# The first attention tiles laid out anew: query quarters on ScalarE's queue, keys without doubling, constants and norms moved, two value products brought forward

## The chip, the cores and the metric

The kernel runs on one core of one Trainium2 chip. The metric is the device time of one execution in microseconds (us); several executions are timed and the median is compared. The core has TensorE (PE, matmuls; its weight loads are listed as PEld), VectorE (DVE), ScalarE (ACT), GpSimd (POOL) and SyncE (SP, which only issues DMAs here). Each engine takes its instructions in program order, and waits on semaphores for other engines and for DMAs.

## What is computed

Three layers follow each other: attention with pooled keys and values, a mixture of experts with top-1 routing, and a maximum of three products with an output product. The change touches the attention alone.

```python
B, H, S, D = 8, 8, 576, 64
Sp = S // 8                                   # 72 pooled keys a head
k_p = k.reshape(B, H, Sp, 8, D).mean(axis=3)
v_p = v.reshape(B, H, Sp, 8, D).mean(axis=3)
scores = np.matmul(q, k_p.transpose(0, 1, 3, 2)) / np.sqrt(D)
attn = softmax(scores)
x = np.matmul(attn, v_p)                      # -> 4608 tokens x 512
xn, en = x / norm(x), expert_emb / norm(expert_emb)
expert = argmax(xn @ en.T / tau)              # then relu(x @ w1[e]) @ w2[e], gated
out = max(y @ m1, y @ m2, y @ m3) @ mo        # y: the gated result
```

## The kernel before

The 4608 tokens are 36 tiles of 128 tokens, nine for two batches; the fifth of the nine holds 64 tokens of each of the two. A loop over `it` in `attention_moe_moe_kernel` runs the tiles as a pipeline written out by hand: in iteration `it` it issues the scores of tile it-1 (`stage_s`, L474, for a mixed tile L460; then VectorE's maximum L489 and subtraction L492), the transposes of exp of tile it-3 (`stage_a`, L505), the query transposes of tile it (`stage_q`, L449), the exp of tile it-1 (`stage_e`, L498), squares of finished rows (L561), and the value products of tile it-4 (`stage_x`, L528, with VectorE's normalisation L538 to L555). After that come the jobs that `todo[it]` lists. Every engine keeps this order, so a job that waits holds up all that stands behind it on its engine.

The jobs prepare a batch's keys and values (`prep_steps`). A batch's 576 pooled rows lie in five pieces of 128, 128, 128, 128 and 64 rows; for keys that are aligned to heads the fourth and fifth have 120 and 72. `pool_k` sums eight rows on VectorE (L300), `pool_k2` does it in three halving steps on GpSimd (L314), `pool_v` and `pool_v1` do the same for values (L324 on GpSimd, L308 on VectorE). `dup_k` writes the keys a second time beside themselves on ScalarE (L318). `trans_k` transposes the pieces on TensorE (L342), and ScalarE copies them into the block-diagonal `kbd` (L346, L347). `spread_v` places the values into `vbd` on GpSimd (L330), `trans_v` transposes them (L376, copied at L378), and `vdot` multiplies them with the normalised expert vectors (L383, then L390 on VectorE). From batch 2 on `trans_kv` transposes keys and values together (L354). From batch 3 on only half of each group of eight rows is loaded, and `add_half` (L207) adds the other half with an adding DMA from GpSimd's queue.

All first loads are issued by SP, in the order expert vectors, keys of batch 0, half the heads of the first queries, values of batch 0, other half, and so on (L245 to L252); the buffers for raw keys and values hold two batches, so a later load waits until a batch has been summed. The PSUM tiles for scores, transposed exp and value products are single, two more (`pq`) serve all other transposes.

The constant steps and the expert vectors' norm are generators whose steps `fill` puts between VectorE's instructions of a tile:

```python
queue.append([chain(en_steps())])
p0[1]()
todo = {0: [lambda: fill(16), p0[2]], 1: [lambda: fill(2), p0[3]], 2: [p0[4]], 3: [p0[5]], 5: [lambda: queue.append([chain(const_steps())])]}
```

Behind the attention follow the routed experts and the last products, both mostly on TensorE.

## Time and profile before

| | |
|---|---|
| median of 3 runs | 1225.17 us (1224.39 to 1225.65) |
| the profiled execution's own time | 1225.17 us |
| span of its profile | 1223.3 us |
| TensorE busy | 98% of the span |
| VectorE, ScalarE, GpSimd busy | 65%, 47%, 25% |

The span goes from the first to the last instruction; the time around it is 1.9 us. "Busy" counts the union of an engine's instructions. Rows of a timeline give the start and the length in us, the engine, the line, the operation with its tiles, how many were merged (x8), and in brackets the idle time before with what ended it. Rows of a table by stretch give for each engine the busy time and the number of instructions, then the granted TensorE clock, the mean share of the 16 DMA engines and GB/s.

### The profile page before, as it was taken

What the parts mean: (1) busy time and instruction counts of PE and PEld (TensorE: products, weight loads), DVE (VectorE), ACT (ScalarE), POOL (GpSimd) and SP (SyncE); (2) the same over time, 40 slices, a digit from 0 to 9 for tenths busy, and PEclk for the clock granted to TensorE, in tenths of its full rate; (3) what the DMA queues carried; (4) which work ended last, traced back from release to release, by engine and by line L of the source; (5) the groups of instructions that cost most, each with busy time, mean ns of one, the idle gap of its engine ahead of it and who ended that gap; (6) DMA issues with size and microseconds to landing.
All of it is one profiled execution on the core that took longest, in us unless ns stands there. A gap on an engine that the chain in (4) does not pass through costs nothing. (4 is left out here: it accounts for less than half of the span.)

```text
span 1223.3 us, 22433 instructions
## 1 busy us (share of the span) xinstructions
PE 1194.4 (98%) x8251; PEld 1149.6 (94%) x8251; DVE 791.5 (65%) x1601; ACT 578.9 (47%) x1040; POOL 308.9 (25%) x441
## 2 busy tenths in 40 slices
PE   6899999999999999999999999999999999999998
PEld 5899999999999999999998998998998998998996
DVE  6878977987799899987844445445455454454450
ACT  4666764455666666666654223323323223223221
POOL 6977734301122121230002102003003003004001
PEclk9999999999999999999999999999999999999999
DMA  9999655418875447555359565574574674674631
GB/s 266 255 255 247 177 185 178 131 20 224 269 254 184 150 166 254 210 180 161 116 157 342 207 241 207 198 249 190 213 250 183 218 258 170 229 262 158 241 144 54
DMA packets 104134, 246.21 MB, mean 201 GB/s; under 512 B 17436, under 2 KB 69962, under 8 KB 95954
## 3 DMA queue, kind: packets, MB, share of 16 engines
q1 hardware_dynamic: 84786, 183.19, 44.1%
q0 software_dynamic: 19232, 61.52, 16.8%
q8 instruction: 67, 1.10, 0.4%
q14 instruction: 49, 0.40, 0.1%
HBM read 252.23 MB, written 46.98 MB: 245 GB/s over the span
## 5 line engine op out<-in xcount | busy, mean ns | idle before, releaser
L1658 PE MATMUL p<-yhi,wt 128*128 128x384 f32 x1512 | 387.6, 336 | 0.5 <-DVE m L1679 0.4
L1658 PEld LDWEIGHTS p<-yhi,wt 128*128 128x128 f32 x1512 | 273.4, 188 | 1.5 <-DVE m L1679 0.7
L1658 PE MATMUL p<-ylo,wt 128*128 128x384 f32 x756 | 254.2, 336 | 0.0
L1666 ACT COPY s<-p 128x384 f32<-128x384 f32 x162 | 77.6, 480 | 222.1 <-PE p L1658 217.6
L1142 PE MATMUL py<-hhi,wlo 128*128 128x256 f32 x576 | 163.2, 283 | 1.6 <-DVE wlo L1074 1.6
L1142 PE MATMUL py<-hhi,whi 128*128 128x256 f32 x576 | 164.7, 286 | 0.0
L1094 PE MATMUL ph<-xhi,whi 128*128 128x256 f32 x576 | 163.9, 285 | 0.7 <-DVE hlo L1110 0.7
L1094 PE MATMUL ph<-xhi,wlo 128*128 128x256 f32 x576 | 163.2, 283 | 0.7 <-DVE wlo L1074 0.7
L1094 PE MATMUL ph<-xlo,whi 128*128 128x256 f32 x576 | 163.1, 283 | 0.0
L1142 PE MATMUL py<-hlo,whi 128*128 128x256 f32 x576 | 163.0, 283 | 0.0
L1658 PEld LDWEIGHTS p<-ylo,wt 128*128 128x128 f32 x756 | 142.2, 188 | 0.5
L1687 DVE TENSOR_TENSOR blk<-p,s 128x384 f32<-128x384 f32 x108 | 59.7, 553 | 112.4 <-PE p L1658 112.4
L1643 POOL DMA_INDIRECT gt<-gbuf,ix x26 | 37.5, 1444 | 308.0 <-DMA ix<-idbuf 301.6
L1142 PEld LDWEIGHTS py<-hhi,wlo 128*128 128x128 f32 x576 | 110.4, 192 | 1.8 <-DVE wlo L1074 1.8
L1094 PEld LDWEIGHTS ph<-xhi,whi 128*128 128x128 f32 x576 | 110.6, 192 | 1.2 <-DVE hlo L1110 1.0
L1094 PEld LDWEIGHTS ph<-xhi,wlo 128*128 128x128 f32 x576 | 110.6, 192 | 0.9 <-DVE wlo L1074 0.9
L1094 PEld LDWEIGHTS ph<-xlo,whi 128*128 128x128 f32 x576 | 110.6, 192 | 0.0
L1142 PEld LDWEIGHTS py<-hlo,whi 128*128 128x128 f32 x576 | 110.5, 192 | 0.0
L1142 PEld LDWEIGHTS py<-hhi,whi 128*128 128x128 f32 x576 | 110.5, 192 | 0.0
L1074 DVE TENSOR_TENSOR wlo<-w2raw,whi 128x1024 fp32r<-128x1024 f32 x84 | 102.3, 1222 | 9.2 <-ACT whi L1072 9.2
L1074 DVE TENSOR_TENSOR wlo<-w1raw,whi 128x1024 fp32r<-128x1024 f32 x67 | 81.9, 1223 | 27.9 <-ACT whi L1072 27.0
L1072 ACT CAST whi<-w2raw 128x1024 fp32r<-128x1024 f32 x88 | 91.7, 1042 | 7.5 <-PE py L1142 4.7
(326 smaller groups left out, 2255.1 us busy)
## 6 DMA issues: line engine op xcount, KB each, us to landing
wt<-wdram SPq DMA_DIRECT2D x51, 1792.0 KB
w1raw<-in_moe_w_dram SPq DMA_DIRECT2D x88, 512.0 KB
w2raw<-in_moe_w_dram SPq DMA_DIRECT2D x88, 512.0 KB
wdram<-wst POOLq DMA_DIRECT2D x9, 1792.0 KB
ybuf<-yo SPq DMA_DIRECT2D x40, 256.0 KB
cvraw<-in_moe_w_dram POOLq DMA_DIRECT2D x36, 256.0 KB
xbuf<-x SPq DMA_DIRECT2D x16, 512.0 KB
yr<-ybuf SPq DMA_DIRECT2D x20, 384.0 KB
```

The lines of the kernel that those rows point to most:

```text
L1072: nc.scalar.copy(hi, src)
L1074: eng.tensor_tensor(lo, src, hi.bitcast(F32), op=A.subtract)
L1094: nc.tensor.matmul(ps[:, f, :], a_[:, c, fs], b_[:, c, :], start=(n == 0), stop=(n == 3 * DC - 1))
L1142: nc.tensor.matmul(py[:, c // 2, (c % 2) * 256 : (c % 2 + 1) * 256], a_[:, f, c * P : (c + 1) * P], b_[:, f, :], start=(piece == 0 and f = ...
L1643: nc.gpsimd.indirect_dma_start(out=gt[g][:, j : j + 1], out_offset=None, in_=gbuf[:, :], in_offset=bass.IndirectOffsetOnAxis(ap=cols[j], a ...
L1658: nc.tensor.matmul(ps, a_, b_, start=(start and c + n == 0), stop=(c == 1 and n == 2), skip_group_check=True)
L1666: nc.scalar.copy(t, ps)
L1687: tt(src, add[0], add[1], op=A.add)
```

## The change

- The expert vectors, the first two query quarters (tiles 0 and 1 of heads 0 to 3, then of heads 4 to 7) and `tau` are issued on ScalarE's queue; SP issues keys, values, and then the queries' other half. The last query group is loaded in two halves, around batch 1's values.
- Keys are transposed without being doubled; both copies into `kbd` read the same 64 PSUM rows. Tile 0 needs only three pieces and the first four heads; the others follow behind its scores. The first keys use the value products' PSUM tile.
- Batch 2's keys are summed three pieces on GpSimd and two on VectorE, and transposed apart from its values; batch 3's adding DMAs are issued behind batch 2's sums of the same kind. Batch 1's first value piece is summed on VectorE.
- Most clears move from VectorE to ScalarE, the first `kbd`'s from GpSimd to VectorE; masks and the other clears of `kbd` come in iteration 2. Most of the norm's steps go to GpSimd. Seven constant steps come first, the others from iteration 8 on.
- In iterations 5 and 6 the exp transposes and value products of the older tiles are issued before the new tile's scores, with batch 1's key transposes between them in iteration 5.

```diff
-        def inverse_norm(pool, ss, n, cols, pre_, tg=None):
+        def inverse_norm(pool, ss, n, cols, pre_, tg=None, eng_=nc.vector):
...
             for _ in range(3):
-                nc.vector.tensor_tensor(t, yf, yf, op=A.mult)
+                eng_.tensor_tensor(t, yf, yf, op=A.mult)
...
+            def load_first(t0, hs, eng):
+                if (0, 0) not in qg:
+                    qg[0, 0] = qp.tile([P, H, 4, D], F32, tag="qgrp", name="qgrp0_0")
+                eng.dma_start(
+                    qg[0, 0][:, hs, t0 : t0 + 2, :].rearrange("p h t d -> p h (t d)"),
+                    q[0, hs, 0:512].rearrange("h (p t) d -> p h (t d)", t=4)[:, :, t0 * D : (t0 + 2) * D],
+                )
...
-            nc.sync.dma_start(en, emb)
+            nc.scalar.dma_start(en, emb)
+            for hs in (slice(0, HP), slice(HP, H)):
+                load_first(0, hs, nc.scalar)
+            nc.scalar.dma_start(rtau, tau.rearrange("(o t) -> o t", o=1).partition_broadcast(P)[:, 0, :])
             kv[0] = [load_rows("kraw", k, 0, KC, True)]
-            load_q(0, 0, lambda: kv[0].append(load_rows("vraw", v, 0, RC, step=2)))
+            kv[0].append(load_rows("vraw", v, 0, RC, step=2))
+            load_first(2, slice(0, H), nc.sync)
             load_q(0, 1)
             kv[1] = [load_rows("kraw", k, 1, KC)]
-            load_q(0, 2)
+            load_q(0, 2, ((0, 2),))
             kv[1].append(load_rows("vraw", v, 1, RC))
...
+            nc.scalar.activation(esq, en, AF.Square, accum_out=ess)
...
+            nc.vector.memset(kbds[0], 0.0)
+            clear(vT[0:D])
+            clear(vT[D:P, 4, R4:P])
+            clear(enT[0:D])
+            clear(vps[0][R4:P, 4, :])
+            clear(aTs[0][R4:P, 4, :])
+            clear(vbds[0][R4:P, SL[4] : NSL, :])
+            clear(aTs[1][R4:P, 4, :])
...
-                vp = kp[:, :, 1, :] if b > 1 else vps[b]
+                vp = kp[:, :, 1, :] if b > 2 else vps[b % 2]
...
+                def first_k():
+                    ps = pb.tile([P, 2, 512], F32, tag="pav", name="ptk0")
+                    flat = ps.rearrange("p a n -> p (a n)")
+
+                    def heads(cs, parts):
+                        for c in cs:
+                            n, col = KC[c], c * P if c < 4 else 512
+                            nc.tensor.transpose(flat[0:D, col : col + n], kp[0:n, c, 0, :], ident[0:n, 0:n])
+                        for h0, h1, col in parts:
+                            src_ = flat[0:D, col : col + (h1 - h0) * SP].rearrange("p (h s) -> p h s", s=SP)
+                            nc.scalar.copy(kb[0:D, h0:h1, 0, :], src_)
+                            nc.scalar.copy(kb[D:P, h0:h1, 1, :], src_)
+
+                    return (
+                        lambda: heads(range(3), ((0, 4, 0),)),
+                        lambda: heads((3, 4), ((4, 7, 4 * SP), (7, 8, 512))),
+                    )
...
                 if b == 1:
                     return [
-                        lambda: (pool_k(0), pool_k(1), pool_k2(KC, 2), pool_v(0, 4, P), pool_v(4, 5, 64)),
-                        lambda: (dup_k(), spread_v(), trans_k(range(4), 0, 7), trans_k([4], 7, 8)),
+                        lambda: (pool_k2(KC, 2), pool_v(1, 4, P), pool_v(4, 5, 64)),
+                        lambda: (pool_k(0), pool_k(1)),
+                        lambda: (trans_k(range(4), 0, 7), trans_k([4], 7, 8)),
+                        lambda: (pool_v1(0), spread_v()),
                         lambda: (trans_v(4, 5), trans_v(0, 4)),
                         vdot,
                     ]
                 if b == 2:
-                    pk = [lambda: (pool_k(0), pool_v(0, 4, P), pool_v(4, 5, 64)), *(lambda c=c: pool_k(c) for c in range(1, 5))]
-                    return pk + [spread_v, lambda: trans_kv(range(4), 0), lambda: trans_kv([4], 4 * P), vdot]
+                    return [
+                        lambda: (pool_k2(KC, 2), add_half(k, 3, kv[3][0])),
+                        lambda: (pool_k(0), pool_k(1)),
+                        lambda: (trans_k(range(4), 0, 7), trans_k([4], 7, 8)),
+                        lambda: (pool_v(0, 4, P), pool_v(4, 5, 64), spread_v(), add_half(v, 3, kv[3][1])),
+                        lambda: (trans_v(4, 5), trans_v(0, 4)),
+                        vdot,
+                    ]
...
-            queue.append([chain(en_steps())])
+            consts, norms = const_steps(), en_steps()
+            for _ in range(7):
+                next(consts)
+            for _ in range(4):
+                next(norms)
+            keys = p0[0]()[1]
+            for _ in range(10):
+                next(norms)
+            make_slots()
+            for _ in norms:
+                pass
             p0[1]()
-            todo = {0: [lambda: fill(16), p0[2]], 1: [lambda: fill(2), p0[3]], 2: [p0[4]], 3: [p0[5]], 5: [lambda: queue.append([chain(const_steps())])]}
+            todo = {
+                0: [keys[0]],
+                1: [lambda: (en_trans(), p0[2]())],
+                2: [lambda: (clear_rest(), p0[3](), make_masks())],
+                3: [p0[4], p0[5]],
+                8: [lambda: queue.append([chain(consts)])],
+            }
...
-                at_ = {1: [2, 4, 6, 7], 2: [5, 6, 6, 7, 7, 7, 8, 9, 10]}.get(b, at_[:4] + at_[5:6])
-                if b >= NFULL:
+                at_ = {
+                    1: [2, 4, None, 6, 7, 7], 2: [6, 8, 9, 6, 11, 12], 3: [9, 10, 12, 13, 14]
+                }.get(b, at_[:4] + at_[5:6])
+                if b > NFULL:
...
-                if 0 <= it - 1 < NT:
+                if it in (5, 6):
+                    stage_a(it - 3)
+                    stage_x(it - 4)
+                    if it == 5:
+                        cur[1][2]()
                     stage_s(it - 1)
...
+                if it == 1:
+                    keys[1]()
+                if it not in (5, 6) and 0 <= it - 3 < NT:
                     stage_a(it - 3)
```

## Rows read from the trace of the kernel before

**Rows 1.** The page: busy time, share and instructions of each engine.
```profile
PE 1194.4 (98%) x8251; PEld 1149.6 (94%) x8251; DVE 791.5 (65%) x1601; ACT 578.9 (47%) x1040; POOL 308.9 (25%) x441
```

**Rows 2.** Busy time by stretch (columns as told above).
```profile
5.00:10.00 5.00, 1.20 (x4) 0.69 (x4) 3.91 (x6) 0.82 (x4) 4.57 (x22) 1.00 1.06 315
...
36.00:52.00 16.00, 13.56 (x115) 12.34 (x114) 15.79 (x48) 7.67 (x19) 14.28 (x26) 1.00 0.97 233
52.00:68.00 16.00, 15.49 (x126) 15.30 (x125) 11.15 (x27) 11.82 (x32) 15.14 (x36) 1.00 0.99 301
```

**Rows 3.** Timeline of TensorE, 0 to 92 us.
```profile
13.01 2.26 PE L474 MATMUL psc<-kbd,qT 128*128 128x144 f32 x8 [0.77 <-ACT qT L450]
...
21.79 1.30 PE L474 MATMUL psc<-kbd,qT 128*128 128x144 f32 x8
...
25.13 1.22 PE L474 MATMUL psc<-kbd,qT 128*128 128x144 f32 x8
26.18 0.71 PE L505 MATMUL paT<-ident,at 128*128 128x128 f32 x5
26.73 0.60 PE L449 MATMUL pqT<-ident,qmix 128*128 128x128 f32 x4
27.16 1.80 PE L528 MATMUL pav<-vbd,aT 128*128 128x146 f32 x12
29.03 0.72 PE L342 MATMUL ptk<-ident,kp 128*128 128x128 f32 x5
...
43.45 1.23 PE L383 MATMUL pd<-enT,vT 128*128 128x16 f32 x10
...
55.86 1.25 PE L474 MATMUL psc<-kbd,qT 128*128 128x144 f32 x8 [0.51 <-ACT qT L450]
...
68.00 0.60 PE L354 MATMUL ptk<-ident,kp 128*128 128x128 f32 x4
```

**Rows 4.** Timeline of VectorE, 0 to 75 us.
```profile
6.85 2.90 DVE L300 TENSOR_REDUCE kp<-kraw 128x64 f32<-128x512 f32 x3 [1.02 <-DMA kraw<-in_k_dram]
...
26.38 0.76 DVE L489 TENSOR_REDUCE mx<-psc 128x8 f32<-128x576 f32 x1 [0.93 <-PE psc L474]
27.25 0.76 DVE L492 TENSOR_TENSOR sh<-psc,mx 128x576 f32<-128x576 f32 x1
29.01 0.17 DVE L538 TENSOR_SCALAR rs<-pav 128x8 f32<-128x8 f32 x1 [1.00 <-PE pav L528]
...
30.30 0.27 DVE L555 TENSOR_REDUCE lg<-dt 128x8 f32<-128x64 f32 x1
```

**Rows 5.** Timeline of GpSimd, 20 to 80 us, DMA issues of its queue among it.
```profile
20.61 1.27 POOL L314 TENSOR_TENSOR kraw<-kraw 128x256 f32<-128x256 f32 x2 [0.51 <-DMA kraw<-in_k_dram]
...
25.18 0.32 POOL L314 TENSOR_TENSOR kp<-kraw 72x64 f32<-72x64 f32 x1
...
29.13 1.26 POOL L324 TENSOR_TENSOR vraw<-vraw 128x256 f32<-128x256 f32 x2 [3.62 <-DMA vraw<-in_v_dram]
...
37.20 2.04 POOL L330 TENSOR_TENSOR vbd<-vp,mslot 128x128 f32<-128x128 f32 x5
...
62.85 2.16 POOL L207 DMA_DIRECT2D kraw<-in_k_dram  x2
64.19 3.07 POOL L207 DMA_DIRECT2D vraw<-in_v_dram  x2
...
73.64 0.49 POOL L314 TENSOR_TENSOR kraw<-kraw 128x128 f32<-128x128 f32 x1 [4.33 <-DMA kraw<-in_k_dram]
...
79.35 0.46 POOL L324 TENSOR_TENSOR vraw<-vraw 128x128 f32<-128x128 f32 x1 [1.56 <-DMA vraw<-in_v_dram]
```

**Rows 6.** Timeline of ScalarE, 8 to 60 us.
```profile
9.93 0.57 ACT L346 COPY kbd<-ptk 64x504 f32<-64x504 f32 x1
...
11.10 0.21 ACT L346 COPY kbd<-ptk 64x72 f32<-64x72 f32 x1
...
28.04 0.69 ACT L498 ACTIVATE at<-sh 128x576 f32<-128x576 f32 x1
```

More of the change, by code (lines that the diff above doesn't have):

```diff
@@ L96, in attention_moe_moe_kernel @@
     ident = cp.tile([P, P], F32, name="ident")
-    make_identity(nc, ident)
     idg = cp.tile([P, NB], I32, name="idg")
@@ L226, in attention_moe_moe_kernel, with load_q @@
             qg = {}
-            def load_q(m, part, between=None):
+            def load_first(t0, hs, eng):
[5 more added lines that the diff above has]
+                )
+            def load_q(m, part, pieces=((0, 4),)):
                 if part == 1:
@@ L235, in load_q @@
                     src = q[2 * m, :, 0:512] if part == 0 else q[2 * m + 1, :, 64:576]
-                    for hs in ((slice(0, HP), slice(HP, H)) if between else (slice(0, H),)):
+                    for t0, t1 in pieces:
                         nc.sync.dma_start(
-                            t[:, hs].rearrange("p h t d -> p h (t d)"), src[hs].rearrange("h (p t) d -> p h (t d)", t=4)
-                        )
-                        if between and hs.start == 0:
-                            between()
+                            t[:, :, t0:t1].rearrange("p h t d -> p h (t d)"),
+                            src.rearrange("h (p t) d -> p h (t d)", t=4)[:, :, t0 * D : t1 * D],
+                        )
@@ new lines, in attention_moe_moe_kernel @@
+            tok_i = rp.tile([P, NT], I32, name="tok_i")
+            for m in range(B // 2):
+                nc.gpsimd.iota(tok_i[:, 9 * m : 9 * m + 4], pattern=[[1, 4]], base=2 * S * m + 1, channel_multiplier=4)
+                nc.gpsimd.iota(tok_i[:, 9 * m + 4 : 9 * m + 5], pattern=[[0, 1]], base=2 * S * m + 513, channel_multiplier=1)
+                nc.gpsimd.iota(tok_i[:, 9 * m + 5 : 9 * m + 9], pattern=[[1, 4]], base=2 * S * m + 641, channel_multiplier=4)
+            i_128 = rp.tile([P, P], I32, name="i_128")
@@ new lines, in attention_moe_moe_kernel @@
+            nc.gpsimd.iota(i_128, pattern=[[1, P]], base=0, channel_multiplier=0)
+            pidx_i = rp.tile([P, 1], I32, name="pidx_i")
+            nc.gpsimd.iota(pidx_i, pattern=[[0, 1]], base=0, channel_multiplier=1)
+            make_identity(nc, ident)
+            esq = kvp.tile([E, DM], F32, name="esq", bufs=1)
+            ess = ap1.tile([E, 1], F32, name="ess")
+            nc.scalar.activation(esq, en, AF.Square, accum_out=ess)
+            zero = ap1.tile([P, 1], F32, name="zero")
@@ L256, in attention_moe_moe_kernel, with clear @@
+            nc.vector.memset(zero, 0.0)
+            def clear(ap):
+                n_, *f_ = ap.shape
+                z_ = zero[0:n_, :]
+                for _ in f_[1:]:
+                    z_ = z_.unsqueeze(1)
+                nc.scalar.copy(ap, z_.to_broadcast(list(ap.shape)))
             kbds = [ap1.tile([P, H, 2, SP], F32, name=f"kbd{i}") for i in range(3)]
@@ L314, in pool_k2 @@
                             nc.gpsimd.tensor_tensor(dst, kt[0:n, c, 0:w, :], kt[0:n, c, w : 2 * w, :], op=A.add)
-                def dup_k():
-                    for c0, c1, n in ((0, 3, P), (3, 4, KC[3]), (4, 5, KC[4])):
-                        nc.scalar.copy(kp[0:n, c0:c1, 1, :], kp[0:n, c0:c1, 0, :])
                 def pool_v(c0, c1, n):
@@ L341, in trans_k @@
                         n = KC[c]
-                        nc.tensor.transpose(
-                            ps[:, col : col + n], kp[0:n, c].rearrange("p two d -> p (two d)"), ident[0:n, 0:n]
-                        )
+                        nc.tensor.transpose(ps[0:D, col : col + n], kp[0:n, c, 0, :], ident[0:n, 0:n])
                         col += n
-                    nc.scalar.copy(kb[0:D, h0:h1, 0, :], ps[0:D, 0:col].rearrange("p (h s) -> p h s", s=SP))
-                    nc.scalar.copy(kb[D:P, h0:h1, 1, :], ps[D:P, 0:col].rearrange("p (h s) -> p h s", s=SP))
+                    src_ = ps[0:D, 0:col].rearrange("p (h s) -> p h s", s=SP)
+                    nc.scalar.copy(kb[0:D, h0:h1, 0, :], src_)
+                    nc.scalar.copy(kb[D:P, h0:h1, 1, :], src_)
                 def trans_kv(cs, r0):
@@ L1506, in attention_moe_moe_kernel @@
                 for j, t in enumerate(at_):
-                    todo.setdefault(t, []).append((b, j))
+                    if t is not None:
+                        todo.setdefault(t, []).append((b, j))
             qorder = [(m, p_) for m in range(B // 2) for p_ in range(3)]
@@ L1551, in attention_moe_moe_kernel @@
                     boundary()
-                if 0 <= it - 4 < NT:
+                if it not in (5, 6) and 0 <= it - 4 < NT:
                     stage_x(it - 4)
```

96 lines of the change are left out of this document (44 added, 52 removed).

## The prediction

> **What bounds the kernel now.** I read the page's head first, then the busy time by stretch, then each engine's instructions in order of time from 0 to 92 us. TensorE is busy for 98% of the span and the others for at most 65% [rows 1]: a microsecond won before TensorE is full is won at the end, unless something later makes it wait again. From 52 us TensorE is busy 15.49 of 16 us; from 36 to 52 only 13.56, while VectorE is busy 15.79 of 16 and GpSimd 14.28 [rows 2]. So the front has three parts: a start in which the first scores wait for the keys until 13.01 us, a stretch to about 52 in which VectorE sets the pace, and then TensorE. The edits end at batch 3, whose first key transposes start at 68.00 [rows 3]; I compare times there. What is done by then is the same work in both kernels, so the difference should last to the end.
>
> I write s, a, q, x for a tile's scores, transposes of exp, query transposes and value products. From one start to the next TensorE spends 1.05 (s), 0.55 (a), 0.43 (q) [rows 3]; x gives its result after 1.8, and the next product can start about 1.65 after it. A tile's maximum and subtraction take 1.63 from start to end (26.38 to 28.01), its normalisation chain 1.56 (29.01 to 30.57), a reduction of one key piece 0.97 (2.90 for three) [rows 4]. On ScalarE a copy of 504 columns takes 0.57, of 72 columns 0.21, an exp 0.69 [rows 6].
>
> **The start.** The score product waits today for all five key pieces, their doubling, 504-column copies, and the query transposes queued behind them. After the edit tile 0 needs three pieces and four heads. The third piece landed at 6.85 (VectorE idled 1.02 for it) [rows 4]. Two query quarters, 0.52 MB, now go out beside it; at 315 GB/s [rows 2] that is 1.7 us. The piece lands between 6.85 and 8.55; I take 8.2, since both quarters are issued in the first two microseconds. VectorE comes to the keys at about 5.5, because four steps of the norm stand ahead and wait for ScalarE's square, itself behind four DMA issues (an estimate); this costs nothing while the third piece is later than 7.4. Reduction 0.97, transpose 0.5 and two copies of 288 columns (0.39 each, interpolated) put s0 at 10.6 (9.8 to 11.0) against 13.01: 2.4 won. The seven clears that now stand first on ScalarE, some 0.2 to 0.7 each by their columns [rows 6], end before the keys are pooled and are hidden; GpSimd's norm steps, before the first values land, likewise.
>
> The first matmuls run at half speed although the granted clock reads 1.00: eight scores take 2.26 at 13.01 and 1.30 at 21.79 [rows 2, 3]. I let the slow part end some way into tile 1. Then s0 2.26, two key transposes 0.6, q1 1.1 and its copy 0.57 give s1 at 15.1, ended at 17.0; plus 1.63, s2 starts at 18.65 against 21.79.
>
> **Where the lead goes.** In iteration 3 the value transposes and the value-expert product now stand together ahead of s3. Scores 1.25, maximum and subtraction 1.63, exp 0.69 (after copies, at 21.75), two copies of the transposed values 0.7, the product 1.2 [rows 3]: s3 at 24.3. Today those transposes lie one iteration earlier and s3 starts at 25.13. The lead is 0.8.
>
> Batch 1's first two key reductions move from iteration 2 to the end of iteration 4, behind x0 on VectorE: x0 at 26.3, its result at 28.15, normalisation to 29.7, two reductions to 31.65, transposes 0.5, two copies 1.14: s4 at 33.3. The two value products brought forward fill TensorE until 31.1; after that it waits 2.2. GpSimd is no later: values of batch 0 spread by 21.2, masks with two large clears and a DMA issue some 4 by estimate, three key pieces 4.9 [rows 5], done at 30.2.
>
> Then q5, a3, x2 (35.4, result 37.2), s5 (37.05 to 38.3). VectorE takes x2's chain first, to 38.8, then tile 5's maximum and subtraction to 40.4, then the value reduction of batch 1, now on VectorE: 41.4. s6 starts at 40.45, x3 ends at 44.1, the transposes 0.7, copies 0.75 and product 1.2 follow, s7 at 46.75.
>
> Batch 2: three of its five reductions leave VectorE (2.9 less), two stand at the end of iteration 8. x4 gives its result at 50.6; its chain ends 52.2, the reductions 54.15, tile 8's maximum and subtraction with a constant step between them 55.8, exp 56.5, a square (priced as an exp) 57.2, two key copies 1.14: s9 at 58.35 against 55.86 [rows 3]. TensorE has done x5 and the key transposes at 54.9 and waits 3.4. It is behind by 2.5 here. s10 and s11 follow at 62.0 and 66.4, with x to 70.0; the value-expert product of batch 2, 1.2, stood before this point today as well. Batch 2 also needs five transposes more, 0.72 [rows 3], inside these times. Batch 3's transposes can start at 71.2 for TensorE: 3.2 later than 68.00.
>
> **The queue behind a wait.** GpSimd's spreading of batch 1's values now waits for that VectorE reduction (41.4), and everything of batches 2 and 3 stands behind it in order: spreading 2.05, batch 2's keys 4.9 (4.89 from 20.61 to 25.50), the issue of batch 3's adding key DMA 1.35, batch 2's values 8.07 (29.13 to 37.20), spreading 2.05 [rows 5]: 59.8. Only then is batch 3's adding value DMA issued. Today such a pair, issued at 62.85 and 64.19, had landed by 73.64 and 79.35 [rows 5]. Values alone take between 5.7 (the difference of the landings) and 10.8 (the first's whole way); I take 8, near the middle, as other loads run at the same time. Landed 67.8, summed 4.0 later (half tiles, half of 8.07): 71.8, bounds 69.5 to 74.6. The same queue order holds back SP: batch 3's value load waits for the reduction at 41.4 too, lands well before 59.8, and delays nothing. The batch's transposes take keys and values together, so TensorE waits for this at 71.2 to 74.6. Against 68.00 the sum is +3.2 by TensorE's own chain and +3.8 by GpSimd's, up to +6.6. GpSimd operations right after a DMA issue ran longer (the pair's issues themselves take 1.3 each), so I take +4.2.
>
> **A rule against the change.** The queries on ScalarE's queue are meant to run beside the keys, but the DMA engines' share is already 1.06 from 5 to 10 us [rows 2]. The Trainium skill (Trainium Kernel Development and Optimization, Key Constraints) says that DMAs of all queues run on the same 16 engines, and a second issuing engine saves issue time alone; by that rule the queries still cost the keys their bytes, which the row's full share agrees with.
>
> **Rivals.**
> - *VectorE's relief counts in full.* The stretch from 36 to 52 is VectorE's; 2.9 us leave it. If TensorE meets no late key copies at s9, it keeps 2.4 of the start and gains 2.9, less 0.72 for transposes: -4.6, 1220.6. It decides at s9: before 53.4 us this holds. For it: VectorE's 15.79 of 16. Against it: two reductions ahead of a maximum in iterations 4 and 8.
> - *Lost and won cancel.* If the third piece lands at 6.85, the slow matmuls end earlier (another 0.6) and batch 3's values land in 5.7, only TensorE's chain is left: +3.2 - 1.4 = +1.8, 1227.0. A change that does nothing measurable belongs here.
> - *The queries hold up the keys.* If the quarters' shorter runs (two tiles side by side where four were) move at half the rate, 0.52 MB costs 3.4; the third piece lands at 10.2, s0 starts at 12.6, all later times move by 2.0: +6.2, 1231.4. For it: the full share [rows 2]; against it: the quarters' bytes are fewer than those of the half that goes out early today. It decides where the third piece lands after 9.5.
>
> **How the numbers follow.** The profiled execution took 1225.17, 1.9 more than its span, and is the median of the runs shown; so the sum is made against 1225.2. My forecast is 1225.2 + 4.2 = 1229.4, own range 1227.7 to 1231.8, chance 0.40. Queries holding up keys 0.12, cancelled 0.22, relief in full 0.26. A change of 0.2%, 2.45 us, is about what a measurement of this kernel can tell from none: faster 0.26, same 0.22, slower 0.52. The range reaches down to 1221, just above the relief case's own middle (leaving some 0.12 below), and up to 1233, above GpSimd's late bound and the queries' price (0.07 left above).
>
> **What would show it.** Right: s0 near 10.6; s3 near 24.3 after a wait for copied values; TensorE waiting for key copies before s4 and s9; GpSimd waiting for a VectorE reduction ahead of batch 1's spreading; batch 3's transposes at 71 to 74. Wrong: s9 before 54, which would mean that VectorE reaches batch 2's reductions earlier than I have it; or batch 3's sums done before 68; or a lead at s0 under 1 us. A difference at batch 3 that does not stand at the end would mean that a later stage waits for something else than TensorE.

## The result and the profile after

The changed kernel takes 1233.93 us in the median of four executions (1231.16 to 1235.90), beside 1225.41 for the kernel before on the same chip: a ratio of 1.007 (95% interval 1.0049 to 1.009), slower by 8.5 us. The profiled execution, the fastest of the four, took 1231.16 with a span of 1229.3, so it is 6.0 slower than the profiled one of before. In a later set of executions beside the kernel before it gave 1.0063 (1.0049 to 1.0077). The forecast was 1229.4 with a range up to 1233: the direction is right, the size is outside.

TensorE's timeline of the changed kernel (start, duration, engine and line, tile names, count, and in brackets the idle time ahead and what ended it) answers to [rows 3]:

```profile
10.54 2.29 PE L535 MATMUL psc<-kbd,qT 128*128 128x144 f32 x8 [0.89 <-ACT kbd L384]
...
17.95 1.22 PE L535 MATMUL psc<-kbd,qT 128*128 128x144 f32 x8 [0.78 <-ACT qT L511]
...
23.35 1.91 PE L535 MATMUL psc<-kbd,qT 128*128 128x144 f32 x8
25.05 1.27 PE L566 MATMUL paT<-ident,at 128*128 128x128 f32 x5
...
30.31 1.88 PE L589 MATMUL pav<-vbd,aT 128*128 128x146 f32 x12 [0.90 <-DVE dt L614]
...
34.18 1.19 PE L521 MATMUL psc<-kbd,qT 128*64 128x144 f32 x14 [0.79 <-ACT kbd L400]
...
41.42 1.22 PE L535 MATMUL psc<-kbd,qT 128*128 128x144 f32 x8 [1.80 <-DVE sh L553]
...
47.62 1.23 PE L535 MATMUL psc<-kbd,qT 128*128 128x144 f32 x8
...
58.98 2.29 PE L535 MATMUL psc<-kbd,qT 128*128 128x144 f32 x8 [3.19 <-ACT kbd L400]
...
65.46 1.19 PE L535 MATMUL psc<-kbd,qT 128*128 128x144 f32 x8
...
74.35 0.63 PE L407 MATMUL ptk<-ident,kp 128*128 128x128 f32 x4
```

These are tiles 0, 2, 3, the exp transposes of tile 1, the value product of tile 1, tiles 4, 6, 7, 9 and 10, and batch 3's first key transposes. Of the kernel before, two rows more are needed, tile 4's scores and tile 7's, from the same view:

```profile
30.92 1.20 PE L460 MATMUL psc<-kbd,qT 128*64 128x144 f32 x14 [0.79 <-ACT kbd L347]
...
45.09 1.22 PE L474 MATMUL psc<-kbd,qT 128*128 128x144 f32 x8 [0.41 <-DVE sh L492]
```

So tile 3 starts 1.8 earlier than before (23.35 against 25.13). From tile 3 to tile 7 pass 24.27 us where 19.96 passed, though both kernels have done the same products by tile 7. From tile 7 to tile 9 pass 11.36 against 10.77, and from tile 9 to batch 3's key transposes 15.37 against 12.14, with five value transposes more in between (0.55). The sum is +6.35 at 74.35, about the span's difference: in this execution most of the loss is made by batch 3 and stays (+7.2 at the last tile's maximum, 178.28 against 171.10).

The busy time by stretch, columns as in [rows 2], shows one part of it: the granted clock.

```profile
24.00:26.00 2.00, 2.00 (x11) 1.95 (x10) 0.71 (x1) 0.00 (x0) 1.92 (x4) 0.50 1.10 276
...
56.00:58.00 2.00, 0.00 (x0) 0.00 (x0) 1.99 (x8) 1.42 (x4) 1.78 (x5) 0.97 0.95 295
58.00:60.00 2.00, 1.02 (x4) 1.03 (x5) 1.26 (x6) 1.33 (x4) 1.84 (x5) 0.50 0.05 15
60.00:62.00 2.00, 2.00 (x11) 1.96 (x10) 0.70 (x2) 0.00 (x0) 2.00 (x5) 0.50 0.52 168
62.00:64.00 2.00, 2.00 (x10) 1.97 (x9) 0.94 (x7) 1.52 (x4) 2.00 (x3) 0.50 1.06 383
```

A clock of 0.50 is 1.2 of 2.4 GHz. It is read from 24 to 26, behind two pauses of 0.53 and 0.82, and from 58 to 64, behind the 3.19 ahead of tile 9. Eight scores then take 2.29 in place of 1.22, and tile 10 starts 6.48 after tile 9, where 3.71 suffices at 2.4 GHz (next section). The Trainium skill (TensorE: Matmul & The Clock Gate, Part 1: The HAM clock gate) says that the array falls to half rate when it idles and returns once it is busy. The rows from 58 on, behind the longest wait, agree; those from 24 to 26 come behind much shorter pauses.

VectorE's timeline of the changed kernel answers to [rows 4]; these are the reductions of batch 1's keys, of its first value piece, and of batch 2's keys:

```profile
30.38 1.99 DVE L340 TENSOR_REDUCE kp<-kraw 128x64 f32<-128x512 f32 x2
...
41.19 1.04 DVE L348 TENSOR_REDUCE vp<-vraw 128x64 f32<-128x512 f32 x1
...
53.03 2.00 DVE L340 TENSOR_REDUCE kp<-kraw 128x64 f32<-128x512 f32 x2
```

And GpSimd's timeline, to [rows 5]: the spreading of batch 1's values, the issue of batch 3's adding value DMA, and the first and fourth of its sums.

```profile
42.31 2.04 POOL L366 TENSOR_TENSOR vbd<-vp,mslot 128x128 f32<-128x128 f32 x5 [5.86 <-DVE vp L348]
...
61.58 2.17 POOL L208 DMA_DIRECT2D vraw<-in_v_dram  x2
...
70.83 0.46 POOL L360 TENSOR_TENSOR vraw<-vraw 128x128 f32<-128x128 f32 x1 [2.97 <-DMA vraw<-in_v_dram]
...
73.80 0.32 POOL L360 TENSOR_TENSOR kp<-vraw 128x64 f32<-128x64 f32 x1
```

GpSimd waits 5.86 for the VectorE reduction, issues batch 3's adding value DMA at 61.58, waits 2.97 for it, and has summed four pieces by 74.12 (the fifth, which the first four transposes do not need, by 74.9). TensorE gets to their transposes at 74.35: two chains end within a quarter of a microsecond of each other.

### The profile page after: what moved, and what is told of

Same layout as the page of the kernel before. It is cut to its first block, busy times and chain, and to the rows that moved or that the text cites. A ratio compares the mean times of both kernels' runs of the same rounds, so it can differ in the third digit from the quotient of the medians.

```text
span 1229.3 us, 22440 instructions
## 1 busy us (share of the span) xinstructions
PE 1196.0 (97%) x8256; PEld 1151.7 (94%) x8256; DVE 787.9 (64%) x1578; ACT 581.5 (47%) x1046; POOL 311.0 (25%) x460
```

## The experiments

Columns: the median with its ratio to the kernel before on the same chip (95% interval), and from the profiled execution, which is one of several, its own time, the start of tile 3, the time from there to tile 7, the start of tile 9, and batch 3's first and, where they are drawn apart, last of four key transposes. "Busy" means added identity transposes. The profiled execution can lie far from the median: that of products_in_place is the slowest of its kernel, that of rearranged_in_place the fastest.

| kernel | us | ratio | profiled | tile 3 | to 7 | tile 9 | batch 3 |
|---|---|---|---|---|---|---|---|
| before | 1225.41 | | 1225.17 | 25.13 | 19.96 | 55.86 | 68.00 |
| after | 1233.93 | 1.007 (1.0049-1.009) | 1231.16 | 23.35 | 24.27 | 58.98 | 74.35 |
| after_again | 1232.91 | 1.0063 (1.0049-1.0077) | 1234.97 | 25.23 | 24.27 | 60.88 | 73.48-75.77 |
| keys2_early | 1233.23 | 1.0066 (1.0053-1.008) | 1234.18 | 25.53 | 24.28 | 58.25 | 73.77-76.19 |
| values1_gpsimd | 1234.60 | 1.0081 (1.0066-1.0095) | 1234.60 | 26.49 | 22.60 | 60.45 | 75.74 |
| both_early | 1228.75 | 1.0027 (1.0018-1.0036) | 1229.67 | 25.81 | 24.27 | 58.53 | 71.27 |
| tensor_kept_busy | 1235.57 | 1.0095 (1.008-1.0111) | 1234.71 | 26.52 | 25.42 | 63.30 | 75.90 |
| start_alone | 1226.55 | 1.0017 (1.0008-1.0026) | 1227.95 | 27.69 | 21.38 | 58.65 | 70.78 |
| queries_on_sp | 1235.78 | 1.0093 (1.0078-1.0109) | 1235.50 | 28.15 | 24.11 | 63.63 | 76.23-77.92 |
| after_start_busy | 1231.41 | 1.0053 (1.0038-1.0068) | 1233.79 | 25.76 | 25.49 | 62.62 | 76.77 |
| before_start_busy | 1224.69 | 1.0001 (0.9992-1.0009) | 1224.25 | 25.45 | 20.31 | 56.02 | 68.15 |
| products_in_place | 1237.37 | 1.01 (1.0085-1.0115) | 1241.53 | 25.21 | 30.75 | 67.33 | 82.67 |
| rearranged | 1226.69 | 1.0018 (1.0009-1.0027) | 1226.33 | 23.53 | 23.97 | 55.94 | 69.16 |
| rearranged_busy | 1226.25 | 1.0009 (1.0-1.0018) | 1227.00 | 22.33 | 23.97 | 54.75 | 67.97 |
| rearranged_in_place | 1226.84 | 1.0021 (1.0008-1.0033) | 1223.52 | 20.85 | 20.15 | 49.86 | 64.01-66.43 |
| rearranged_in_place_busy | 1226.52 | 1.001 (0.9998-1.0022) | 1226.28 | 21.40 | 20.12 | 50.39 | 65.09-67.52 |
| values3_early | 1224.15 | 0.9993 (0.9983-1.0004) | 1224.29 | 23.79 | 20.12 | 52.77 | 66.04 |
| values3_early_busy | 1222.31 | 0.9979 (0.997-0.9988) | 1223.05 | 21.50 | 20.41 | 50.77 | 64.14 |

**The two late chains.** The changed kernel again; batch 2's key reductions and transposes an iteration earlier; batch 1's first value piece back on GpSimd; and both.

```diff
-  2: [6, 8, 9, 6, 11, 12]                      # keys2_early, both_early
+  2: [6, 7, 8, 6, 11, 12]
-  pool_k2(KC, 2), pool_v(1, 4, P), ...         # values1_gpsimd, both_early
+  pool_k2(KC, 2), pool_v(0, 4, P), ...
-  lambda: (pool_v1(0), spread_v()),
+  spread_v,
```

after_again: 

> The changed kernel once more, as the control of this set. In its first profile batch 3's key transposes started at 74.35 us (before: 68.00), TensorE waited 3.2 us ahead of tile 9's scores, and the granted clock was 0.50 from 59 to 64 us. Theory A (the wait and the half clock after it): the same wait and a half clock again, in every execution, though its length may differ. Theory B (GpSimd's order of work): batch 3's value sums end at about 74 again and decide where the transposes start. Both: 1231 to 1236.

keys2_early: 

> The changed kernel with batch 2's two VectorE key reductions one iteration earlier (7 instead of 8) and its key transposes in iteration 8 instead of 9. Theory A: the wait ahead of tile 9's scores goes (those scores at about 56 instead of 59), the granted clock stays at 1.00 there, and TensorE is ready for batch 3's transposes at about 69 to 70; 4 to 5 us less than the changed kernel, some 1228. Theory B: batch 3's value sums still end at about 74, TensorE waits there instead, and the time stays within 1 us of the changed kernel.

values1_gpsimd: 

> The changed kernel with batch 1's first value piece summed on GpSimd again, so that spreading batch 1's values waits for no VectorE reduction. GpSimd then starts batch 2's sums at about 40 instead of 44.3, and batch 3's value sums end at about 70 instead of 74.9. Theory A: no change of the time beyond 1 us, since tile 9's wait and the half clock stay. Theory B: batch 3's transposes start at 70 to 71, 3 to 4 us less than the changed kernel.

both_early: 

> Both edits together. Theory A: as with the earlier key reductions alone. Theory B: as with the value piece on GpSimd alone. If both hold each other up (each alone moves little because the other ends at the same time): only this one moves, batch 3's transposes start at about 70, and the time is 4 to 5 us less than the changed kernel, some 1227 to 1229.

Alone, neither edit makes the kernel faster (1.0066 and 1.0081 beside 1.0063); together they give back some 4 us of 8 (1.0027). With keys2_early tile 9 no longer waits, though tile 10 now waits 2.02 for VectorE, and batch 3's transposes wait for GpSimd's sums instead; with values1_gpsimd those sums are early (four done by 67.31), and TensorE waits 3.20 ahead of tile 9. That shows that the two chains end together. The repeat of the changed kernel also shows that the half speed does not always come in the same place. TensorE's timeline of after_again, tiles 9 and 10, the last of batch 3's transposes and tile 12:

```profile
60.88 1.25 PE L535 MATMUL psc<-kbd,qT 128*128 128x144 f32 x8 [3.22 <-ACT kbd L400]
64.59 1.19 PE L535 MATMUL psc<-kbd,qT 128*128 128x144 f32 x8
...
75.77 0.33 PE L407 MATMUL ptk<-ident,kp 128*128 128x128 f32 x1 [0.48 <-POOL kp L360]
75.93 1.63 PE L535 MATMUL psc<-kbd,qT 128*128 128x144 f32 x8
```

Here tile 9 follows as long a wait at full speed, 3.71 ahead of tile 10; but tiles 0 to 3 all ran at half speed, and the clock fell again behind the waits for GpSimd, from 76 on (0.57 from 76 to 80).

**The clock.** values1_gpsimd with 24 transposes that fill the wait ahead of tile 9, and the changed kernel and the kernel before with 30 and 39 of them in the pauses of the start.

```diff
+  for _ in range(24):                          # behind batch 2's last key transpose
+      nc.tensor.transpose(ps[:, P : 2 * P], ident, ident)
```

tensor_kept_busy: 

> This is the kernel of values1_gpsimd with 24 identity transposes added on TensorE behind batch 2's key transposes, so that TensorE works through its wait ahead of tile 9's scores; their results go to columns that nothing reads. Theory (it is the idling of 3.2 us ahead of tile 9 that brings the half clock after it): tile 9's scores start where they did, at about 60.5, but take 1.25 for eight in place of 2.29, tile 10 starts near 63.5 in place of 66.85, batch 3's key transposes near 72.5 in place of 75.74 with GpSimd's sums already done at 68, and the time falls by some 3 us, to about 1231.5. Rival one (the clock falls for another reason, such as the work since the start): the granted clock still reads 0.50 after 60 and the time stays at 1234.6. Rival two (the added transposes delay tile 9 themselves): its scores start after 61.5 and the time is above 1235.

after_start_busy: 

> This is the changed kernel with 30 identity transposes added on TensorE in the gaps of the start (11 ahead of the first query transposes, 8 between and behind the first key transposes, 3 and 4 ahead of the scores of tiles 1 and 2, 4 ahead of tile 2's query transposes); their results are thrown away. Theory (the matmuls of tiles 0 to 3 run at half speed because TensorE pauses between them, and that takes the lead of the start): eight scores take 1.25 in place of 2.29 from tile 0 or 1 on, tile 3 starts near 22 in place of 23.35 to 25.23, but the end gains at most 2, since batch 1's value reduction on VectorE and GpSimd's queue behind it still end near 73: 1230 to 1232 beside 1233 without. Rival (the half speed of the start does not come from the pauses): eight scores of tiles 0 to 2 still take 2.2 or more and the time is 1232 to 1236. Second rival (the start's half speed is all that was lost): 1226 or less.

before_start_busy: 

> This is the kernel before the change with 39 identity transposes added in the gaps of its start (28 ahead of the first key transposes, 2, 3, 3 and 3 ahead of the fifth key transpose, of tile 0's query transposes and of the scores of tiles 0 and 1). Theory (the clock is a limit of the start in both kernels): tile 0's and tile 1's scores take 1.25 in place of 2.26 and 2.29, tile 3 starts about 2 earlier than 25.13; from 36 to 52 VectorE is full, so at most half of it stays: 1223 to 1224.5. Rival (VectorE's full stretch takes all of it): batch 3's key transposes at 68.0 as before, the time within 0.7 of the kernel before.

In the profile of tensor_kept_busy the granted clock stays 1.00 from 36 to 90, and from tile 9 to batch 3 pass 12.60 in place of 15.29: the half speed behind tile 9's wait cost 2.7 in values1_gpsimd. That the added transposes prevent it is not shown by one profile, since after_again and queries_on_sp have full speed there without them. Yet the time did not fall. Tile 9 starts at 63.30 and the time is above 1235, where the second rival put them; but from tile 7 to tile 9 pass 11.36 as without the added transposes, so they did not delay it. In this execution the clock read 0.55 from 25 to 30 and tile 7 came 2.8 later; which executions lose where, the profiles of single executions cannot settle. In the start the added transposes bring tile 0 to full speed: eight scores take 1.25 in all four versions of the changed start with them, 2.29 in all without. TensorE's timeline of after_start_busy, tile 0 and then tile 2's query transposes, added transposes and scores:

```profile
10.07 1.25 PE L545 MATMUL psc<-kbd,qT 128*128 128x144 f32 x8 [0.89 <-ACT kbd L390]
...
17.06 0.66 PE L518 MATMUL pqT<-ident,qgrp 128*128 128x128 f32 x4 [2.07 <-DMA qgrp<-in_q_dram]
17.56 0.60 PE L287 MATMUL psc<-ident 128*128 128x128 f32 x4
18.45 2.29 PE L545 MATMUL psc<-kbd,qT 128*128 128x144 f32 x8 [0.29 <-ACT qT L519]
```

TensorE waits 2.07 for the queries of tile 2 and falls to half speed behind that. In the ten profiles of the changed start in which TensorE waits for these queries, their transposes start between 15.98 and 17.41, so a faster tile 0 does not bring tile 2 forward by as much. The time is not told apart from that without the added transposes (1.0053 against 1.0063 and 1.007). The kernel before gains nothing by the same means (1.0001). Its tile 2 starts 0.8 earlier (21.01 for 21.79), its tile 3 0.3 later: VectorE then waits for batch 1's keys, whose sums stand ahead of tile 2's maximum. Here are VectorE's reduction of the keys and, from TensorE's timeline, tile 3's scores, in before_start_busy:

```profile
21.74 2.03 DVE L300 TENSOR_REDUCE kp<-kraw 128x64 f32<-128x512 f32 x2 [0.79 <-DMA kraw<-in_k_dram]
...
25.45 1.22 PE L480 MATMUL psc<-kbd,qT 128*128 128x144 f32 x8 [1.19 <-DVE sh L498]
```

**The start.** All edits of the start with the schedule of batches 1 to 3 as it was; and the changed kernel with the first query quarters behind the keys on SP's queue.

```diff
-  for hs in (slice(0, HP), slice(HP, H)):      # queries_on_sp: moved behind
-      load_first(0, hs, nc.scalar)             # the loads of batch 0's keys,
+      load_first(0, hs, nc.sync)               # issued by SP
```

start_alone: 

> This is the changed start (loads, keys without doubling, constants, norms, clears) with the schedule of batches 1 to 3 as it was before: two products not brought forward, batch 1's reductions in iteration 2, batch 2's five reductions on VectorE, batch 3's adding DMAs where they were. Theory (the lead of the start is gone by tile 3, and the loss is in the schedule of batches 1 and 2): tile 0 starts near 10 in place of 13.01, tile 3 between 23.5 and 25.5, tile 9 between 54.5 and 56.5, and the time is 1223.5 to 1226. Rival (the start's edits themselves bring the loss, through the undoubled keys and the moved masks): tile 9 starts after 58 and the time is above 1229. Second rival (the lead lasts and is only spent later): tile 9 before 54 and the time below 1223.

queries_on_sp: 

> This is the changed kernel with the first two query quarters issued on SyncE's queue behind batch 0's keys; the embedding and the scalar stay on ScalarE's queue. Theory (the quarters cost the keys their bytes, whichever engine issues them beside the keys): the third key piece lands near 6.9 to 7.3 in place of 8.16, tile 0 starts up to 1 us earlier unless the queries are now the later of the two, and the end moves by less than 1 us, since tile 9 waits for VectorE and batch 3 for GpSimd all the same: 1231.5 to 1234. Rival (the queue itself, not the bytes, sets when the keys land): the piece stays at 8.1 to 8.2. Second rival (the start's lead reaches the end after all): 1 us or more faster at the end, 1231.9 or less.

start_alone lost 2.4 us; its median is half a microsecond above its theory's range. Its tile 9 lies where the first rival put it, after 58, its time well below that rival's 1229. Tile 0 starts at 9.74, 3.3 earlier than before, and tile 3 at 27.69, 2.6 later: behind the now adjacent value transposes TensorE waits 2.37 for their copies, and tiles 2 and 3 run at half speed, as TensorE's timeline of start_alone has it:

```profile
25.94 1.90 PE L436 MATMUL pd<-enT,vT 128*128 128x16 f32 x10 [2.37 <-ACT vT L431]
27.69 2.27 PE L527 MATMUL psc<-kbd,qT 128*128 128x144 f32 x8
```

The copies are late because VectorE is: with the schedule of before, batch 1's key reductions stand ahead of tile 2's maximum, and VectorE's timeline shows it idle until those keys have landed:

```profile
21.04 1.99 DVE L340 TENSOR_REDUCE kp<-kraw 128x64 f32<-128x512 f32 x2 [3.10 <-DMA kraw<-in_k_dram]
22.94 0.76 DVE L542 TENSOR_REDUCE mx<-psc 128x8 f32<-128x576 f32 x1
```

So the new start gains three microseconds at tile 0 and with this schedule loses them by tile 3; by the medians some 6 us are left for the schedule of batches 1 and 2. With the changed schedule the lead at tile 3 is 1.8 in after's profile and gone in six others (25.21 to 26.52, against 25.13 before). With the quarters on SP, the third key piece was reduced from 7.68 on, neither the theory's 6.9 to 7.3 nor the rival's 8.1 to 8.2, against 8.16 in the profile of after and no wait for it at all in after_again; the price of the queries' bytes in the keys' landing, 1.7 us in the prediction, is lost in the scatter between executions. The Trainium skill (Trainium Kernel Development and Optimization, Key Constraints) says that DMAs issued from different engines' queues run on the same 16 DMA engines; what sharing them costs the keys, no run here shows. The queries themselves were late: tile 0 started at 12.58, and the median's ratio is 0.003 above after_again's (0.0023 above after's, whose interval overlaps). Its time lies above the theory's range as well.

**The schedule of batches 1 and 2.** rearranged takes keys2_early, batch 1's key reductions in iteration 3 and its value reduction in 5, the masks earlier, and the first value-expert product behind tile 3's scores. products_in_place undoes, in the changed kernel, the two products brought forward; rearranged_in_place does so in rearranged. Both also put batch 1's value transposes into iteration 6 in place of 7. The edits are abridged:

```diff
-  1: [2, 4, None, 6, 7, 7], 2: [6, 8, 9, 6, 11, 12]
+  1: [2, 3, None, 5, 7, 7], 2: [6, 7, 8, 6, 11, 12]     # rearranged
...
-  if it in (5, 6): stage_a(it - 3); stage_x(it - 4); ...; stage_s(it - 1)
+  1: [2, 3, 4, 5, 6, 7], 2: [6, 7, 8, 6, 11, 12]        # rearranged_in_place
+  1: [2, 4, 4, 6, 6, 7], 2: [6, 8, 9, 6, 11, 12]        # products_in_place
```

rearranged: 

> This is the changed kernel with batch 2's key reductions one iteration earlier (as keys2_early), batch 1's key reductions in iteration 3 and its first value reduction in iteration 5 in place of 4 and 6, the masks made earlier on GpSimd, and batch 0's value-expert product moved out of iteration 3, behind tile 4's exp products' preparation. Theory (TensorE's wait ahead of tile 9 and GpSimd's wait for VectorE's value reduction are the two causes, and the transposes of values ahead of tile 3 cost the start's lead): GpSimd's spreading of batch 1's values starts before 40, batch 3's adding value DMA is issued before 58 and its values are summed by 70, tile 9 starts at 56 to 58 without a wait, tile 3 at 22 to 24, batch 3's key transposes at 68 to 70: 1224 to 1227.5. Rival (VectorE is too full for either to come earlier without pushing a maximum back): tile 9 after 59 or batch 3's transposes after 71.5, and the time is 1228.75 or more, as both_early.

rearranged_busy: 

> This is the kernel of rearranged with the same 30 identity transposes in the gaps of the start. Theory (with both late chains moved earlier, what the start wins reaches the end): tile 3 starts near 22 in place of 23.53, batch 3's key transposes near 67.5 in place of 69.16, the time 1223.5 to 1225.5. Rival one (tile 2 waits for its queries and batch 1's stretch for VectorE whatever the clock does): batch 3's transposes stay at 68.5 to 69.5, 1225.5 to 1227.5. Rival two (the added work in the start is in the way): above 1227.5.

products_in_place: 

> This is the changed kernel with one part undone: the value products of tiles 1 and 2 (and their exp transposes) stand behind the scores of iterations 5 and 6 again, as before the change, and batch 1's key transposes at the end of iteration 4. Theory (the two products in front only fill a wait that the late key reductions of batch 1 make): TensorE now waits some 3 for key copies ahead of tile 4, the 0.90 (first product waits for the other's reading) and the 1.80 ahead of tile 6 are gone, tile 7 starts within 1 of 24.3 behind tile 3 as now, and the time stays at 1232 to 1235. Rival (the products in front are themselves the loss of 2.7 between tiles 3 and 7): tile 7 starts 21.5 to 22.5 behind tile 3 and the time is 1229.5 to 1231. Second rival (they are worth more than they cost): tile 7 is 26 or more behind tile 3, the time above 1236.

rearranged_in_place: 

> This is the kernel of rearranged with the value products of tiles 1 and 2 back in their places as before the change and batch 1's value transposes back in iteration 6. Theory (with batch 1's keys reduced in iteration 3, no wait is left for the products to fill, and bringing them forward only makes TensorE wait 0.90 for the product's single buffer and 1.81 behind VectorE's queue): tile 7 starts 21 to 22 behind tile 3 in place of 23.97, batch 3's key transposes at 66.5 to 68 in place of 69.16, the time 1223 to 1225, at or under the kernel before. Rival (VectorE's queue holds the same stretch whatever the order): tile 7 some 24 behind tile 3, 1226 to 1227.

rearranged_in_place_busy: 

> This is the kernel of rearranged_in_place with the 30 identity transposes in the gaps of the start. Theory (the start's half speed costs what the end can now give back): tile 3 near 22, batch 3's key transposes at 65.5 to 67, the time 0.5 to 1.5 under rearranged_in_place. Rival (VectorE, or the landing of batch 3's values, sets the pace again by then): within 0.4 of it.

In the changed kernel the time rises without the products in front, as the second rival has it. TensorE stands still ahead of batch 1's key and value transposes, in TensorE's timeline of products_in_place:

```profile
33.39 0.27 PE L396 MATMUL ptk<-ident,kp 128*64 128x128 f32 x1 [2.67 <-DVE kp L340]
...
49.27 1.03 PE L429 MATMUL ptv<-ident,vp 128*64 128x128 f32 x4 [2.56 <-DVE vp L348]
```

It falls to half speed behind both. Only the first wait is the gap that the products fill; the second comes from the value transposes, which in iteration 6 stand ahead of their reduction's end. How much of the 6.5 from tile 3 to tile 7 belongs to the products alone, this run does not show. With the keys reduced in iteration 3 it is the other way round: 20.15 from tile 3 to tile 7 with the products in their old places, 23.97 with them in front, where TensorE waits 0.90, 0.79 and 1.81 around them (a further 0.67 belongs to the value transposes). Both hold the first value-expert product of 1.2, which in the kernels before and after stands ahead of tile 3; like for like they are 19.0 and 22.8 beside their 19.96 and 24.27. From tile 7 to tile 9 both take 8.4 to 8.9, against 10.77 before: the changed handling of batch 2's keys is worth 2 us once their reductions stand early. That need not be VectorE's relief. In that stretch TensorE waits, in the kernel before, for GpSimd's value sums, since keys and values are transposed together there, as TensorE's timeline of before has it:

```profile
51.27 0.33 PE L354 MATMUL ptk<-ident,kp 128*128 128x128 f32 x1 [1.15 <-POOL kp L324]
```

No run parts VectorE's relief from the separate transposes. In the profile of rearranged_in_place tile 9 starts 6.0 earlier than before, 4.3 of it from tile 3. Of that lead 4.0 are left at the first of batch 3's four transposes (the five value transposes and a wait of 0.88 for VectorE lie between), and 1.8 behind the last, since TensorE waits for GpSimd's sums. In its TensorE timeline, tile 9 and the first and last of the four:

```profile
49.86 1.19 PE L535 MATMUL psc<-kbd,qT 128*128 128x144 f32 x8
...
64.01 0.33 PE L407 MATMUL ptk<-ident,kp 128*128 128x128 f32 x1 [0.25 <-POOL kp L360]
...
66.43 0.33 PE L407 MATMUL ptk<-ident,kp 128*128 128x128 f32 x1 [0.48 <-POOL kp L360]
```

That execution, 1223.52, is the fastest of eleven, which reach to 1233.14; their median, 1226.84, is above the theory's 1223 to 1225, although the steps came as it had them. rearranged lies inside its range. With the start's pauses filled, neither moves clear of the scatter (1226.25 and 1226.52): there the theories on the start's clock failed.

**The adding DMA.** On top of rearranged_in_place, batch 3's adding value DMA is issued beside the key DMA, ahead of batch 2's value reductions on GpSimd.

```diff
-  lambda: (pool_k2(KC, 2), add_half(k, 3, kv[3][0])),
+  lambda: (pool_k2(KC, 2), add_half(k, 3, kv[3][0]), add_half(v, 3, kv[3][1])),
...
-  lambda: (pool_v(0, 4, P), pool_v(4, 5, 64), spread_v(), add_half(v, 3, kv[3][1])),
+  lambda: (pool_v(0, 4, P), pool_v(4, 5, 64), spread_v()),
```

values3_early: 

> This is the kernel of rearranged_in_place with the adding DMA of batch 3's values issued beside that of its keys, ahead of batch 2's value reductions on GpSimd instead of behind them. Theory (GpSimd's queue is what is left: it waits 2.78 for that DMA ahead of batch 3's value sums, and TensorE's transposes then wait 0.25 and three times 0.48 for the sums): no wait for the DMA is left, the sums are done by 64, batch 3's key transposes go through in one piece at 63.5 to 64.5 in place of 64.01 to 66.43, and the time falls by some 2, to 1223 to 1225. Rival (the DMA's issue only moves into the way of batch 2's value reductions, which end as much later): batch 3's sums end at 66 again and the time is within 1 of 1226.84. Second rival (the spread of the times comes from the start's clock, which this does not touch): the highest times stay above 1229 whatever the median does.

values3_early_busy: 

> This is the kernel of values3_early with the 30 identity transposes in the gaps of the start. Theory (where TensorE no longer waits at batch 3 the clock stays up there too, and only the start's half speed is left for the added transposes to take away): 0.5 to 1.5 under values3_early and a narrower spread. Rival (queries and VectorE set the start's pace): within 0.4 of it.

GpSimd no longer waits for the DMA, the four transposes go through in one piece, and the median falls by 2.7 against rearranged_in_place, to that of the kernel before. In its profile the transposes start at 66.04 and not at 63.5 to 64.5, as this execution's tiles 0 and 2 ran at half speed (tile 3 at 23.79 for 20.85). With the pauses of the start filled the median is 1222.31, the one version that beats both kernels (0.9979, 0.997 to 0.9988); it is 1.8 under values3_early, with intervals that just overlap. Its times spread over 2.7 us, those of values3_early over 7.3. TensorE's timeline of values3_early_busy, tile 9 and batch 3:

```profile
50.77 1.19 PE L545 MATMUL psc<-kbd,qT 128*128 128x144 f32 x8
...
64.14 0.81 PE L413 MATMUL ptk<-ident,kp 128*128 128x128 f32 x4
```

Of the 3.9 that it leads by at batch 3, 2.0 are left at the last tile's maximum (169.13 against 171.10). By the starts of the scores 1.0 goes ahead of tile 21, where TensorE waits for GpSimd's sums among the key transposes, and 1.2 ahead of tile 27, behind waits of 0.34 and 0.47 for VectorE; some is regained between.

## Why the prediction was right and wrong

**Right.** Tile 0 (10.6, measured 10.54), the value-expert product's wait for copies ahead of tile 3, VectorE's reductions behind the value product's chain in iterations 4 and 8, TensorE's wait of 3.4 ahead of tile 9 (3.19, at 58.98 for 58.35), GpSimd's wait for VectorE's value reduction, and both chains' lateness at batch 3. Of the rivals, VectorE's relief in full needed tile 9 before 53.4 and is out; "lost and won cancel" needed an early landing and is out (its sum takes off 1.4, though its text names 1.35 and another 0.6). "The queries hold up the keys" asked for a third piece after 9.5; it was reduced at 8.16. Tile 0's agreement is luck in part. It needed the third piece late, at 8.16 for 8.2; in the ten other profiles with this start, the queries on ScalarE's queue and no transposes added in it, tile 0 starts between 9.73 and 10.13.

**The steps that failed** are two, one in each chain. In TensorE's it is "s10 and s11 follow at 62.0 and 66.4", and with it "s4 at 33.3": from tile 3 on every matmul was priced at full speed, although the plan itself put waits of 2.2 and 3.4, and one for copied values, into TensorE's stream. Measured, tile 10 came 6.48 after tile 9 and not 3.65, and tile 4's scores 10.83 after tile 3's and not 9.0. values1_gpsimd, whose tile 3 ran at full speed, took 9.17 for the latter, and after_again 3.71 for the former. So half speed was worth 1.7 and 2.8 in the profiled execution. The rest of TensorE's chain was close: tile 4 to tile 7 13.44 against 13.45, tile 7 to tile 9 11.36 against 11.6. With the two terms, 71.2 becomes 75.7; the start ran 0.95 ahead of the forecast, and 74.35 was measured.

In GpSimd's chain it is "Landed 67.8, summed 4.0 later", a sum that was too small by 3.1 and ended past its bounds: the spreading began 0.9 later than forecast (42.31 for 41.4), the key DMA's issue took 2.31 for the 1.35 priced, so the value DMA was issued at 61.58 for 59.8, and its data were first used 9.25 after the issue, for a priced 8. Four of the five sums were done at 74.12 and the fifth at 74.9, for 71.8 and a bound of 74.6. Each chain ends at the measured point by itself, so neither term alone is the whole miss. I took "+4.2" from the later of two chains; it should have been asked what removing one of them leaves. keys2_early and values1_gpsimd show that removing one alone gives nothing back, both_early that removing both gives back 4 of 8.

The profiled execution lies inside the prediction's own range; the median is 2.8 above it, and why is only in part known. after_again's profiled execution took 3.8 more than this one. It is 1.9 later at tile 3, behind four tiles at half speed, 2.0 at tile 26 and 3.5 at tile 29. So the start's half speed can make some 2 of such a difference; that it does so in the others is argued, not shown, and what comes behind tile 26 stays open.

**Not seen at all**: that the products brought forward fill a gap which the late key reductions make, and cost 3 us or more where there is no such gap (23.97 against 20.15). The prediction followed the order as written and priced most of its waits rightly, but did not ask what the order would be worth with the reductions elsewhere. That is where the change's own gain lay hidden: 3.1 to 6.0 us at tile 9 (52.77 and 49.86 against 55.86), of which the best version keeps 2.5 to the end.

## What to carry to other kernels

Where a change puts waits into TensorE and TensorE sets the pace, price the work behind them at both clocks. Where two chains end at the same point, undo both before judging either: each alone showed nothing here, together 4 us. A work item moved to fill a gap is worth at most the gap; move the late input first, and the filler may turn into the wait.

## What the hardware showed

The granted clock reads 1.00 from 9 to 15 us, while eight scores take 2.29 (10.54) and not 1.22; in the profiles here a reading of 0.50 stands beside slow matmuls only behind a first stretch at full speed. The Trainium skill (TensorE: Matmul & The Clock Gate, Part 1, Seeing it yourself) warns that recorded clock events are not always to be trusted; here too the durations have to be read beside them. Waits of 3.19 to 3.22 in the same place, ahead of tile 9, dropped the clock in four profiles (after, values1_gpsimd, after_start_busy, products_in_place) and not in two (after_again, queries_on_sp).

A GpSimd operation that follows a DMA issue is recorded longer: the pair of half sums behind the issue at 49.14 takes 2.14 and the next 1.27. The prediction read this as a slower operation. But the records overlap: the issue runs to 51.45, the pair from 50.60 to 52.74, and from 51.45 on only 1.29 are left. The rows fit an issue that takes 2.31 and sums that take as long as ever.

The way of an adding DMA is uneven. From issue to first use batch 3's values took 9.25 in after and 8.76 in both_early, where GpSimd waited for them, and at most 6.26 in values1_gpsimd (57.78 to 64.04), where it did not.
